# A windowed-attention and relu-squared kernel on one core: a new hand-written emission order, and the last pair's product and stores cut differently

## The chip, the core and the metric

The kernel runs on one NeuronCore of a Trainium2 chip. The metric is the device time of one execution in microseconds (us); lower is better. The core has TensorE (PE, matrix products; its weight loads are shown apart as PEld), VectorE (DVE), ScalarE (ACT), GpSimd (POOL) and SyncE (SP). SP, ACT and POOL can each issue DMAs, which all run on the core's 16 DMA engines.

## What is computed

Attention with a sliding window of 128 keys and 4 sink keys over 4 batches of 8 heads, 768 positions, head size 64; then a two-layer network with a squared relu:

```python
scores = where(keep, q @ k.T / sqrt(64), -1e9)      # keep: key < 4, or 0 <= query - key < 128
x = softmax(scores) @ v                             # [4*768, 512]: heads side by side
g = maximum(x @ w_in, 0) ** 2                       # w_in  [512, 2048]
out = g @ w_out                                     # w_out [2048, 512], out float32
```

## The kernel before

**Tiles and stages.** A batch is 6 tiles of 128 rows, taken as three pairs (256 rows). Per batch come: q and k turned so that the head size lies on the partitions (batches 0 and 1 by PE transposes, batches 2 and 3 by DMA transposes that SP issues, L389), scores (L529), exp on ACT (L549), masks (L558, L561 on DVE, L198 on POOL), sink scores and values (L490, L583), values (L608), the norm (L623, L624), x turned again (L653 or, for batches 2 and 3, L639), layer 1 (L685; in batches 2 and 3 `layer1_fast`, L825, with seven block products for eight), relu and square, and layer 2 (`layer2`, L914, for the first two pairs of batch 0; otherwise `layer2_fast`, L1024). `layer2_fast` makes the four quarters c, b, d and a of a pair's output from seven products of eight matmuls, with four block sums on DVE ahead of them (L982) and additions on the way out (L1049, L1065, L1072). The fast forms need sums of weight blocks: three `weights_in` into `qkT` (L735, free once all scores of batch 2 are done), two in place in `w_in_sb` (L730), and four of `w_out` (L955).

**What sets the order.** Nothing is scheduled by machine. `Plan` (L75) holds 898 numbered operations with the engines that each may run on. The string `ORDER` (L18 to L57) lists them once each; a word is an operation's number, the engine that it is given (p PE, v DVE, a ACT, g POOL, s SP) and, for some PE words, `+n`: so many dummy matmuls ahead (`warm`, L168 to L172). `Plan.run` (L87) emits the words one by one. Each engine works through its own words strictly in that order. An operation that takes a buffer gets the one that was freed first in the emission (`free[s.pool].pop(0)`), so the order also decides who shares a buffer with whom: 4 slots of two PSUM banks for products, 15 for middle results, 2 for output tiles.

**Words that the prediction speaks of** (the same number is the same operation before and after, up to 877):

| word | operation |
|---|---|
| 0, 1 | constants; zero and one fills of batch 0 (L213 to L215), which the v loads of batch 0 wait for |
| 3, 4, 5, 6 | identity, triangles, bias tiles, head rows (POOL, L224 to L249) |
| 8 to 15 | float32 loads of q and k of batch 0, issued by SP (L313) |
| 19, 20, 22, 23 | v loads of batch 0, tiles 0 to 3 (POOL, L339) |
| 21, 24, 25, 26 | the four quarters of w_in (POOL, L278); they arrive as bf16 |
| 27 to 30 | q and k of batch 0, tiles 4 and 5 (POOL, L328) |
| 74, 79 | a regroup of q (L182 on POOL, L181 on DVE or ACT); sink values (L473) |
| 119 | mask of batch 0, second pair |
| 160, 166, 172 / 163, 169, 175, 181 | layer 1 of batch 0, first pair / second pair, 16 matmuls each; 160 and 163 use the first quarter of w_in, 166 and 169 the second, 172 and 175 the third, 178 and 181 the fourth |
| 125, 127 | x of batch 0, second pair, turned |
| 229, 246, 294, 312, 270 | norm, mask (batch 1), evacuation, the first product of layer 2's third pair of batch 0, scores |
| 395, 421 | sink scores of batch 2; scores of batch 2 |
| 425, 606, 607 to 613 | mask of batch 2; loads of q, k and v of batch 3 |
| 477, 480 | copy u of batch 1's second pair (L1038 to L1043, helper L181); a product that waits for it |
| 506, 507, 508 / 509, 510 | `weights_in` into qkT / in place |
| 526, 527, 540, 541 | products that read 509 and 510 |
| 638, 654, 662 | scores of batch 3 |
| 863 to 877 | layer 2 of batch 3, second pair; 874 its last product, 875 the middle quarters, 876 the first quarter, 877 its store of 512 KB |
| 878 to 892 | layer 2 of batch 3, last pair ("tail"), up to its last quarter |

**The tail before.** Product a of the last pair (893) is 16 matmuls into two halves of a slot of its own. `first_quarter` (895, L1084) copies one half on DVE and the other on ACT, and issues a 64 KB store for each, from SP and from ACT. `store_rest` (896, L1102) issues the two middle quarters as two stores of 128 KB on SP; `store_last` (897, L1111) the last quarter, 128 KB, on SP. The second pair's store 877 stands ahead of 896 on SP.

Of the kernel before, what the change touches and what calls it, by code (L numbers as in the profile page):

```python
# [12 lines left out]
FP32 = mybir.dt.float32  # L13
# [2 lines left out]
ALU = mybir.AluOpType  # L16

ORDER = """  # L18
8s 0v 6g 4g 3g 9s 10s 11s 55v 5g 12s 13s 14s 56v 1v 19g 57p 59a 58p+3 60v 20g 21g 22g 67a 23g 103p+8 68v 61v 62v 7a
69p 71v 63p+1 70p 73v 72a 83p 85a 64p 104p 75p 107a 15s 74g 105a 65v 79g 66v 91p 93a 77v 76p 78v 80v 84p 86a 87p+1 92p  # L20
89p 94a 114p 116a 24g 25g 81p 82a 26g 27g 28g 88v 106v 95p 97p 115p 120p 129g 90v 99p 98v 96v 101p+1 29g 30g 117v 109p
118a 102v 110p 111v 121p 100a 160p 119v 123p 31g 32g 108v 33g 122v 124v 112p 113v 166p 125p 126a 127p 128v 172p 175p
173a 176v 177v 163p 164a 165a 169p 161v 133p 135a 134a 167v 170a 34g 181p 35g 147p 171v 149a 148p 151a 2v 182v 178p
179a 130p 132a 131a 36g 37g 38g 39g 40g 297p 298p 138p 152v 183a 139p 150v 142a 143v 136p 137a 299p 300p 301p 140a
141v 41g 42g 43g 44g 45g 46g 168a 47g 144p 153p 154p 155v 145p 146v 302p 303p 156p 48g 158p 159a 282v 305a 304p 49g
50g 51g 157v 184p 16s 283v 284v 285v 174v 187p 306a 162a 185a 52g 53g 188a 196p 212g 200p 201p 54g 363g 364g 197p 199v
208p 209p 210a 381s 203v 193p 202v 198v 211v 223p 194a 195v 186v 226a 189v 224a 225v 227v 190p 242p 191a 286p 204p
206v 205p 287p 207v 245a 243a 257p 258v 365g 366g 367g 234p 237a 238g 259v 288p 289p 235a 368g 369g 370g 371g 372g
373g 236g 180v 192v 254p 213v 308v 216p 217a 255v 256v 219a 290p 291p 262p 265a 307s 228p 292p 293p 263a 266g 214p
246v 309v 384s 310v 311v 229v 260p 374g 261a 382s 244v 218v 383s 386s 294v 295a 385s 264g 215a 312p 314a 313p 220v  # L30
239p 270p 273a 271a 274g 387s 240p 241v 375g 315p 318v 221p 222v 316p 267p 247p 248p 249v 230p 232p 233v 268p 319p
250p 269v 251v 252p 253v 317a 320p 231a 404p 405a 275p 17s 407a 376g 377g 378g 323p 272v 276p 321v 322v 336p 337a 388s
338a 277v 324v 325a 348p 339p 340a 349v 406v 278p 390s 280p 279v 281a 408v 330p 379g 380g 604g 605g 350a 331a 397p
398a 399v 606g 400a 393v 401v 391s 342p 343a 421p 422a 345p 346v 389s 392s 296s 409p 623s 333p 410v 347v 402p 403v
412s 424a 344a 411s 624s 326s 607g 625s 608g 609g 610g 611g 612g 425g 334a 341a 327p 328v 413p 416a 613g 18s 627s 332v
329a 335v 449v 468v 470v 450v 360p 361a 414a 415g 351p 352a 357p 358a 469v 471v 431p 432a 472p 473p 394v 434a 435g
362a 475p 433v 474v 478v 439p 442a 440a 395p 507v 396a 417g 508v 506v 476p 354p 477v 359a 426p 355a 511a 353a 356a
436p 437p 438v 451v 452v 479p 480p 418p 423g 427p 428v 514v 453p 455a 419p 420v 454p 456p 457p 622s 458a 638p 614g
512v 628s 641a 459v 629s 487v 639a 488v 481v 482v 483p 484v 640v 513v 460p 461p 626s 444p 462v 485a 463v 441g 642v
443g 615g 616g 635v 654p 657a 655a 445p 464p 446v 530p 532a 486s 465v 466a 531p 533v 509v 489v 662p 665a 534p 447s  # L40
429s 516p 517p 518v 491p 492p 494p 493a 535v 515v 430s 510v 490v 663a 448s 519v 617g 656g 520p 521v 536p 537p 495p
498p 496a 643p 497v 500v 644v 544v 546v 522p 658g 523p 618g 538a 540p 619g 633s 541p 542v 539a 524a 525a 499p 502p
526p 527p 543a 545v 501v 503v 630s 467s 547v 576p 562p 577p 528v 578a 579v 580p 563p 666g 634g 504a 564a 566p 590p
591p 565v 581v 567v 548p 550v 549p 568p 505s 592a 593v 582p 569p 583p 594p 529a 596p 551v 570a 572p 573p 584a 585a
690v 595v 597p 574v 552p 554p 553v 586p 587p 598a 599a 588v 632s 691v 555p 556a 620g 600p 631s 636p 637a 601p 575a
602v 664v 694p 558p 559p 645p 648a 692v 646a 560v 693v 695p 649v 697p 696a 700v 589a 667p 672p 675a 647v 668p 669v
698p 650p 651v 653s 603a 699a 701p 702p 703v 621g 673a 561v 571v 557a 704v 709v 680p 676g 681a 682g 710v 659p 674g
652s 705p 711v 660p 661v 683a 713p 715v 714p 716p 717p 712v 720p 706v 707a 719v 708s 684g 747a 718v 749v 748v 677p
685p 678p 679v 721p 686p 687v 766p 768a 752p 753p 722v 723v 728v 767p 770p 689s 754a 756p 729v 724p 755v 750v 757v
732p 733p 734a 758p 759p 769v 730v 731v 771v 671s 688s 772p 735p 773p 751v 760a 725v 726a 762p 763p 764v 736p 739p  # L50
738v 670s 780v 782v 783v 774a 776p 777p 737a 778v 798p 800a 799p 740p 741v 742v 801v 727s 784p 786a 785p 787v 743p
781v 744v 812p 813p 802p 761a 814a 745a 746s 788p 779v 826p 804p 803v 789v 765a 827p 775v 805p 790p 816p 815v 818p
840v 791p 806a 808p 809p 817v 841v 828a 819p 830p 810v 829v 831v 792a 842v 794p 795p 796v 820a 822p 823p 824v 793a
811a 832p 833p 834a 835a 844p 846v 843v 807a 845p 821v 847p 850v 849a 836p 837p 838v 825a 839v 797a 878v 879v 848p
851p 852p 855p 882p 883p 859v 853v 854v 860v 856v 857v 858s 885p 863p 864p 866p 884v 888v 880v 887a 865a 881v 886p
889p 861v 867p 862v 869v 891v 892v 897s 868v 870p 872v 873v 871p 874p 875v 876a 877s 890p 894v 893p 895v 896s
"""  # L57


# [47 lines left out]
def kernel(  # L107
# [851 lines left out]
    def layer2_fast(b, u):  # L959
# [48 lines left out]
            else:  # L1008
                touch((b, u), e, ins, HOME[name][0], alone=alone)

        def product(n, name, lhs, rhs, first, after, takes=(), reads=()):
            def run(e):
                if n == 0:
                    bank_t["y", b, u] = tile_of(bs, "py", [128, 2, 2, 256], FP32)
                if tail and n == 2:
                    bank_t["ya", b, u] = tile_of(ys, "ya", [128, 2, 2, 256], FP32)
                y = region(name)
                x = lhs if not isinstance(lhs, str) else t_[lhs]
                w_ = wt_sb[rhs] if isinstance(rhs, int) else rhs
                for c in range(2) if tail and name == "a" else (None,):  # L1020
                    for i in range(HB):
                        y_ = y if c is None else y[:, c, :]
                        r_ = w_[:, i, :] if c is None else w_[:, i, 128 * c:128 * c + 128]
                        ins = nc.tensor.matmul(y_, lhsT=x[:, i, :], rhs=r_, start=(first or tail and n == 2) and i == 0,  # L1024
                                               stop=i == HB - 1, skip_group_check=not (first or tail and n == 2))
                        use(name, e, ins, c)
# [38 lines left out]
            nc.vector.tensor_tensor(out=t_["x"], in0=t_["x"], in1=t_["u"], op=ALU.add)  # L1065
        P.group = ("ev", b, u)
        e4 = op("last_quarter", "dve", last_quarter, after=[ex, eu])
        p2 = product(6, "a", a12, w(1, 0), False, [u0] + high)

        def middle(e):  # L1070
            o, y = bank_t["osb", b, u], bank_t["y", b, u]
# [10 lines left out]
            return pairs[:, i, c0:c1]  # L1082

        def first_quarter(e):  # L1084
            o, y = bank_t["osb", b, u], region("a")
            if not tail:
                use("a", e, copy(e, o[:, 0, :], y))
                return
            h = tile_of(half_, "half", [128, 128], FP32)
            use("a", "dve", copy("dve", o[:, 0, 0:128], y[:, 0]), 0)  # L1090
            use("a", "act", copy("act", h, y[:, 1]), 1)
            nc.sync.dma_start(out=rows(0, 0, 128), in_=o[:, 0, 0:128])
            nc.scalar.dma_start(out=rows(0, 128, 256), in_=h)
        half_ = Slot("w2", 1)
        e1 = op("first_quarter", "dve" if tail else "act dve", first_quarter, takes=[half_] if tail else [],
                after=[p2, em], reads=[ys, os_] if tail else [bs])
# [5 lines left out]
        def store_rest(e):  # L1102
            o = bank_t["osb", b, u]
            if b not in FAST or not u:
                nc.sync.dma_start(out=pairs.rearrange("p i m -> p (i m)")[:, 256:768],
                                  in_=o[:, 1:3, :].rearrange("p c m -> p (c m)"))
                return
            for i in range(2):
                nc.sync.dma_start(out=rows(i, 256 - 256 * i, 512 - 256 * i), in_=o[:, 1 + i, :])

        def store_last(e):  # L1111
            nc.sync.dma_start(out=rows(1, 256, 512), in_=bank_t["osb", b, u][:, 3, :])
        if tail:
            op("store_rest", "sp", store_rest, after=[em, e4], dma=2.0)
            op("store_last", "sp", store_last, after=[e4], dma=2.0)
        else:
            op("store", "sp", store, after=[em, e1, e4], reads=[os_], dma=2.0)


# [107 lines left out]
```

## Time and profile before

| | |
|---|---|
| runs | 217.24, 217.24 and 215.4 us; median 217.24 us |
| the profiled execution | 216.34 us; its span in the trace is 214.6 us |
| granted TensorE clock | 1.0 in every slice |
| PE / DVE / ACT / POOL busy | 93% / 80% / 60% / 48% of the span |
| DMA | 26.09 MB moved, 122 GB/s on average |

A span starts with the first instruction and ends with the last. In rows of the timeline the first two numbers are start and length in us; a bracket at the end names the idle time ahead of the instruction on its engine and what ended it. "x8" means eight instructions merged. In rows of the DMA view the last number is the median time in us from a DMA's issue to its landing.

### The profile page before, as it was taken

The page shows a single profiled execution, that of the slowest core. Times are in us where ns is not written, and L with a number is a line of the kernel's source. Part 1 is how long each engine was busy: PE and PEld are TensorE (multiplying, and loading weights), DVE is VectorE, ACT ScalarE, POOL GpSimd, SP SyncE. Part 2 cuts the span into 40 slices and gives each one's busy share as a digit, 9 for nine tenths or more (in the row PEclk, how much of TensorE's full clock was granted, in tenths as well). Part 3 has the DMA queues.
Part 4 walks back from the last instruction along what each step waited for, and adds up shares of the span by engine and source line. Part 5 has one row for each costly group of instructions (what it writes and reads, how often), then busy time and mean ns, then how long its engine had stood idle before and what let it go on. Part 6 is the DMA issues. An engine that isn't in the chain of part 4 may idle for free.

```text
span 214.6 us, 5463 instructions
## 1 busy us (share of the span) xinstructions
PE 199.2 (93%) x2270; PEld 163.4 (76%) x2270; DVE 171.6 (80%) x311; ACT 128.2 (60%) x165; POOL 102.8 (48%) x139
## 2 busy tenths in 40 slices
PE   1887899999998999999989998999999999999991
PEld 1546898579754785459768888998887999998981
DVE  4887176396799685479898999989998989998971
ACT  2582159845866536978992755678962245695001
POOL 5799265498979999032599199000244000000000
PEclk9999999999999999999999999999999999999999
DMA  5999999999999999997527949980022340200204
GB/s 164 270 154 189 179 190 213 170 153 146 104 214 131 165 125 159 177 178 148 127 53 49 147 97 81 225 97 0 3 49 100 75 124 5 99 0 3 98 27 171
DMA packets 93881, 26.09 MB, mean 122 GB/s; under 512 B 86816, under 2 KB 91552, under 8 KB 93856
## 3 DMA queue, kind: packets, MB, share of 16 engines
q0 software_dynamic: 69248, 12.59, 78.3%
q1 hardware_dynamic: 24424, 13.07, 26.3%
q8 instruction: 18, 0.29, 0.5%
q10 hardware_dynamic: 184, 0.07, 0.1%
q14 instruction: 7, 0.06, 0.1%
HBM read 27.30 MB, written 6.29 MB: 156 GB/s over the span
## 4 chain that ended last, share of the span: by engine, by line
PE 68%; DVE 15%; DMA 6%; POOL 3%; issue 3%; ACT 2%; DVEq 0%; ACTq 0%
PE py L1024 20%; PE pm L685 17%; PE pm L825 15%; DMA w_in_sb<-in_moe_w_in_dram 5%; PE py L914 4%; PE po L608 4%; PE ps L529 4%; DVE sg L982 3%; PE pt L425 2%; POOL v L339 2%; DVE qkT L735 2%; DMA qr<-in_k_dram 1%; DVE w_in_sb L730 1%; DVE r L893 1%; DVE gT_sb L982 1%
## 5 line engine op out<-in xcount | busy, mean ns | idle before, releaser
L198 POOL TENSOR_SCALAR_AFFINE_SELECT expm<-expm 128x512 bf16<-128x512 bf16 x38 | 32.0, 876 | 43.8 <-ACT expm L549 43.8
L549 ACT ACTIVATE expm<-ps 128x1024 bf16<-128x1024 f32 (+1 forms) x48 | 43.8, 958 | 11.3 <-PE ps L529 11.1
L685 PE MATMUL pm<-xT,w_in_sb 128*128 128x256 bf16 (+1 forms) x320 | 44.6, 295 | 1.0 <-DMA w_in_sb<-in_moe_w_in_dram 1.0
L685 PEld LDWEIGHTS <-w_in_sb 128*128 128x128 bf16 x320 | 34.3, 114 | 7.7 <-DMA w_in_sb<-in_moe_w_in_dram 1.3
L1024 PEld LDWEIGHTS <-gT_sb 128*128 128x128 bf16 x336 | 30.8, 98 | 4.8 <-issue 1.2
L1024 PEld LDWEIGHTS <-sg 128*128 128x128 bf16 x240 | 22.4, 98 | 5.0 <-DVE xn_sb L624 1.2
L825 PE MATMUL pm<-xs,w_in_sb 128*128 128x128 bf16 (+1 forms) x256 | 24.0, 246 | 0.8 <-DVE w_in_sb L730 0.8
L696 ACT ACTIVATE r<-pm 128x1024 bf16<-128x1024 f32 x17 | 17.4, 1026 | 10.6 <-PE pm L685 10.4
L339 POOL DMA_DIRECT2D v<-in_v_dram x24 | 21.9, 923 | 2.6 <-DVE v L215 1.7
L825 PEld LDWEIGHTS <-w_in_sb 128*128 128x128 bf16 x256 | 21.7, 114 | 1.2 <-DVE w_in_sb L730 0.9
L1024 PE MATMUL py<-wt,sg 128*128 128x256 bf16 x160 | 20.8, 273 | 1.3 <-DVE xn_sb L624 0.9
L1024 PE MATMUL py<-wt,gT_sb 128*128 128x256 bf16 x160 | 20.8, 273 | 0.7 <-DVE u L181 0.7
L328 POOL DMA_DIRECT2D qn<-in_q_dram x20 | 17.8, 902 | 6.1 <-DMA w_out_sb<-in_moe_w_out_dram 5.3
L847 ACT ACTIVATE gT_sb<-r 128x1024 bf16<-128x1024 bf16 x18 | 18.7, 1057 | 0.3 <-DVE r L893 0.2
L179 ACT ACTIVATE osb<-py 128x256 f32<-128x256 f32 (+1 forms) x17 | 7.0, 420 | 19.7 <-DVE osb L1072 10.3
L1024 PE MATMUL py<-w_out_sb,gT_sb 128*128 128x256 bf16 x144 | 18.7, 273 | 0.0
L328 POOL DMA_DIRECT2D qn<-in_k_dram x20 | 17.8, 907 | 1.0 <-issue 1.0
L624 DVE TENSOR_TENSOR xn_sb<-po,rc 128x512 bf16<-128x512 f32 (+1 forms) x28 | 17.2, 615 | 1.0
L893 DVE CUSTOM_DVE_ANT_1 r<-pm,t 128x1024 bf16<-128x1024 f32 x12 | 14.6, 1220 | 2.7 <-PE pm L825 2.5
L881 ACT ACTIVATE r<-pm 128x1024 bf16<-128x1024 f32 x12 | 12.1, 1020 | 7.1 <-PE pm L825 7.0
L825 PEld LDWEIGHTS <-qkT 128*128 128x128 bf16 x192 | 16.1, 114 | 0.2 <-issue 0.2
L866 DVE TENSOR_TENSOR t<-t,pm 128x512 f32<-128x512 f32 x24 | 15.9, 680 | 0.3
(94 smaller groups left out, 328.8 us busy)
## 6 DMA issues: line engine op xcount, KB each, us to landing
out_dram<-osb SPq DMA_DIRECT2D x11, 512.0 KB, 4.6
v<-in_v_dram POOLq DMA_DIRECT2D x24, 128.0 KB, 6.1
qn<-in_k_dram POOLq DMA_DIRECT2D x20, 128.0 KB, 6.9
qn<-in_q_dram POOLq DMA_DIRECT2D x20, 128.0 KB, 6.5
w_in_sb<-in_moe_w_in_dram POOLq DMA_DIRECT2D x4, 512.0 KB, 9.3
w_out_sb<-in_moe_w_out_dram POOLq DMA_DIRECT2D x4, 512.0 KB, 10.5
qr<-in_k_dram SPq DMA_DIRECT2D x4, 256.0 KB, 4.9
qr<-in_q_dram SPq DMA_DIRECT2D x4, 256.0 KB, 4.7
```

The lines of the kernel that those rows point to most:

```text
L198: nc.gpsimd.affine_select(out=e_tile, in_=e_tile, compare_op=ALU.is_ge, fill=fill, base=i - 1, pattern=[[0, n], [1 if i else -1, 128]], ch ...
L328: nc.gpsimd.dma_start(out=qn_t[b, ti][:, t, :].rearrange("p (h d) -> p h d", d=D), in_=(q, k)[ti][b, :, 128 * t:128 * t + 128, :].rearrang ...
L339: nc.gpsimd.dma_start(out=v_sb[b % 2][:, t, :, 0:D], in_=v[b, :, 128 * t:128 * t + 128, :].rearrange("h p d -> p h d"))
L549: nc.scalar.activation(out=x[:, :, o:512], in_=bank_t["s", b, s, m][:, :, o:512], func=AF.Exp, scale=scale)
L624: touch(("po", b, s, m0), e, nc.vector.tensor_tensor(out=xn_sb[:, 2 * s:2 * s + 2, :].rearrange("p i (j q h d) -> q p j i h d", j=2, q=2, ...
L685: nc.tensor.matmul(pm[:, i, :], lhsT=w_in_sb[:, fb // 4, kb, fb % 4:512:4], rhs=xT[:, c0 // 256:(c0 + cw) // 256, kb, :], start=(kb == 0), ...
L696: nc.scalar.activation(out=o, in_=h, func=AF.Relu)
L825: touch(tag, e, nc.tensor.matmul(y[:, bk, i, :], lhsT=weights(name, f0 + i, a), rhs=rhs[:, a, :], start=fresh and i == 0 and a == 0, stop= ...
L847: nc.scalar.activation(out=d, in_=x, func=AF.Square)
L866: touch(tag, e, nc.vector.tensor_tensor(out=T["t"], in0=T["t"], in1=T["y"][:, bk], op=ALU.subtract), bk)
L893: touch(tag, e, nc.vector._custom_dve(TENSOR_ADD_SAT, out=r.rearrange("p b n c -> p b (n c)"), in0=T["y"].rearrange("p b n c -> p b (n c)" ...
L1024: ins = nc.tensor.matmul(y_, lhsT=x[:, i, :], rhs=r_, start=(first or tail and n == 2) and i == 0, stop=i == HB - 1, skip_group_check=not ...
```

## The change

The words of `ORDER` are put in another order over the whole kernel, and 77 operations below 878 go to another engine or carry another number of dummy matmuls (18 dummies in all, 14 before). Of the layer 2 code only the last pair changes: its last product becomes two operations (893, 894) of eight matmuls, one for each half; the halves are copied by an operation each (898, 900) into the output tile, and no longer into a tile of their own; the two middle quarters leave in one DMA of 256 KB (897); and each of the four stores may be issued by SP or ACT. The words that the prediction speaks of, engine by engine:

```diff
 POOL, start
-6g 4g 3g 5g 19g 20g 21g 22g 23g 74g 79g 24g 25g 26g 27g 28g 129g 29g 30g
+4g 3g 5g 6g 19g 20g 21g 22g 23g 24g 25g 26g 27g 28g 79g 119g 29g 30g
 DVE, start
-0v 55v 56v 1v 60v 68v 61v 62v
+0v 1v 55v 67v 59v 71v 60v 61v 72v 73v 65v 74v
 PE, start
-57p 58p+3 103p+8 69p 63p+1 70p 83p ... 160p 123p 112p 166p 125p 127p 172p 175p 163p 169p 133p 181p
+57p 69p+11 58p 70p+1 103p+1 83p ... 160p 110p 121p 112p 123p 166p 125p 127p 172p 163p 181p 169p 130p
 around 246 and 477
-246v ... 507v 508v 506v 477v
+246g ... 451v 508v 635v 507v ... 485v 506v   (and 477a, on ACT, behind 434a 396a 432a)
 ACT between 421p and 395p
+422a 424a 349a 279a 347a 337a 338a 361a 416a 352a 414a 511a 358a
 POOL, loads of batch 3
-606g 607g 608g 609g 610g 611g 612g 425g 613g
+606g 425g 607g 608g 609g 610g 611g 612g 613g
 PE, end
-837p 848p 851p 852p 855p 882p 883p 885p 863p 864p 866p 886p 889p 867p 870p 871p 874p 890p 893p
+837p 847p 848p 851p 852p 855p 882p 883p 885p 886p 889p 863p 864p 866p 867p 890p 893p 870p 871p 874p 894p
 DVE, end
-861v 862v 869v 891v 892v 868v 872v 873v 875v 894v 895v
+862v 865v 891v 892v 869v 895v 872v 873v 875v 876v
 ACT and SP, end
-865a 876a                    858s 897s 877s 896s
+868a 897a 898a 900a          858s 899s 896s 901s 877s
```

In the new order 895 is the middle quarters of the last pair, 896 the store of its last quarter, 897 that of its middle quarters, 898 and 900 the copies of the halves of product a, 899 and 901 their stores. The code:

```diff
-        p2 = product(6, "a", a12, w(1, 0), False, [u0] + high)
+        if tail:
+            p2s = [product(6, "a", a12, w(1, 0), False, [u0] + high, cs=(c,)) for c in range(2)]
+        else:
+            p2 = product(6, "a", a12, w(1, 0), False, [u0] + high)
...
+        def half(c):
+            def run(e):
+                use("a", e, copy(e, bank_t["osb", b, u][:, 0, 128 * c:128 * c + 128], region("a")[:, c]), c)
+            return run
...
+        def queue(e):
+            return nc.scalar if e == "act" else nc.sync
+
+        def store_middle(e):
+            o, two = bank_t["osb", b, u], rows(0, 256, 512)
+            two = bass.AP(two.tensor, two.offset, [list(two.ap[0]), [128 * DM - 256, 2], [1, 256]])
+            queue(e).dma_start(out=two, in_=o[:, 1:3, :])
...
         if tail:
-            op("store_rest", "sp", store_rest, after=[em, e4], dma=2.0)
-            op("store_last", "sp", store_last, after=[e4], dma=2.0)
+            op("store_last", "sp act", store_last, after=[e4], dma=2.0)
+            op("store_middle", "sp act", store_middle, after=[em], dma=2.0)
+            for c in range(2):
+                ec = op("half", "dve act", half(c), after=[p2s[c]])
+                op("store_half", "sp act", store_half(c), after=[ec], dma=2.0)
```

More of the change, by code (lines that the diff above doesn't have):

```diff
@@ L24 @@
[L24 to L28, printed above, removed]
@@ L57 @@
+863p 865v 864p 866p 868a 867p 891v 890p 893p 892v 870p 869v 871p 874p 895v 872v 897a 898a 899s 896s 894p 900a 901s
+873v 875v 876v 877s
 """
@@ L1019, in run @@
                 w_ = wt_sb[rhs] if isinstance(rhs, int) else rhs
-                for c in range(2) if tail and name == "a" else (None,):
+                for c in cs if tail and name == "a" else (None,):
                     for i in range(HB):
@@ L1084, in first_quarter @@
         def first_quarter(e):
[L1085 to L1096, printed above, removed]
+            use("a", e, copy(e, bank_t["osb", b, u][:, 0, :], region("a")))
+        def half(c):
+            def run(e):
+                use("a", e, copy(e, bank_t["osb", b, u][:, 0, 128 * c:128 * c + 128], region("a")[:, c]), c)
+            return run
         def store(e):
```

88 lines of the change are left out of this document (45 added, 43 removed).

## The prediction

> **What bounds the kernel now.** I read the page's head, the list of PE's waits, the timeline at each longer wait, then the DMA view around the loads concerned. First the page: span, busy time, and the share of each engine in the chain that ended last.
>
> ```profile
> span 214.6 us, 5463 instructions
> PE 199.2 (93%) x2270; PEld 163.4 (76%) x2270; DVE 171.6 (80%) x311; ACT 128.2 (60%) x165; POOL 102.8 (48%) x139
> PE 68%; DVE 15%; DMA 6%; POOL 3%; issue 3%; ACT 2%; DVEq 0%; ACTq 0%
> ```
>
> PE bounds it: 93% busy and 68% of the chain. The diff takes no product away, so PE's 199.2 us stay (four more dummies fall where PE waits), and only the rest, 214.6 − 199.2 = 15.4 us, can shrink. The list of PE's waits says where some of it lies (us in total, times, longest).
>
> ```profile
> PE pt L425 <- DVE qs L181: 4.8, 2, 4.6
> PE py L1024 <- DVE xn_sb L624: 0.9, 1, 0.9
> PE pm L825 <- DVE w_in_sb L730: 0.8, 1, 0.8
> PE py L1024 <- DVE u L181: 0.7, 1, 0.7
> ```
>
> 4.6 pass before the first k tile is cast; the diff leaves those loads alone. The other three sum to 2.4 us. The timeline of the start shows more.
>
> ```profile
> 3.79 1.29 DVE L181 CAST qs<-qr 128x512 bf16<-128x512 f32 x2 [2.14 <-DMA qr<-in_k_dram]
> 6.05 0.10 DVE L215 MEMSET v<- 128x48 bf16 x1
> 6.45 2.16 POOL L339 DMA_DIRECT2D v<-in_v_dram  x2 [1.66 <-DVE v L215]
> 9.35 1.80 POOL L339 DMA_DIRECT2D v<-in_v_dram  x2
> 11.71 1.81 POOL L473 TENSOR_TENSOR vs<-vs_in,head_rows 32x130 bf16<-32x130 f32 x4
> 13.47 2.31 POOL L278 DMA_DIRECT2D w_in_sb<-in_moe_w_in_dram  x3
> 16.03 1.02 ACT L549 ACTIVATE expm<-ps 128x1024 bf16<-128x1024 f32 x1 [0.21 <-PE ps L529]
> 21.98 1.94 PE L685 MATMUL pm<-xT,w_in_sb 128*128 128x256 bf16 x16 [0.89 <-DMA w_in_sb<-in_moe_w_in_dram]
> 24.52 7.18 PE L685 MATMUL pm<-xT,w_in_sb 128*128 128x256 bf16 x64 [0.15 <-DMA w_in_sb<-in_moe_w_in_dram]
> ```
>
> PE is dense only from 24.52 on: both bracketed waits end when a quarter of w_in lands. These quarters are issued by POOL at 13.47, 14.24 and 15.0 (the x3 row). So the kernel is a start set by loads, a dense run with a few stalls, and a tail.
>
> **The change part by part.**
>
> *The start.* Issue to landing, in the DMA view at 13.4, 15.7 and 10.2 us (last number, a median):
>
> ```profile
> w_in_sb<-in_moe_w_in_dram POOLq DMA_DIRECT2D x1, 512.0 KB, 8.5
> w_in_sb<-in_moe_w_in_dram POOLq DMA_DIRECT2D x1, 512.0 KB, 12.1
> v<-in_v_dram POOLq DMA_DIRECT2D x2, 128.0 KB, 7.9
> ```
>
> The second quarter lands at 13.47 + 8.5 = 21.97, the third at 24.5 (PE's wait), the fourth at 15.0 + 12.1 = 27.1: 2.5 apart, one transfer behind another. The last v load ahead of them (issued about 10.25) lands at 18.2, 3.77 before 21.97; 3.77 − 2.5 leaves a gap of about 1.2 in the stream. Two edits feed it earlier. First, 1v stands ahead of the casts on DVE, in the 2.14 us in which DVE has nothing to do; POOL, free at 6.45 − 1.66 = 4.79, can then issue v at once, 1.66 earlier. Second, 24g to 26g no longer stand behind 74 and 79g (2.3 us from 11.15 to 13.47), so they follow 23g directly: issued some 4 us earlier in all, ahead of need, and the gap closes. Upper bound of the gain: 1.66 + 1.2 = 2.9. Attention cuts it: the exp of the second pair ended at 17.05 and gets a regroup of about 0.6 ahead of it; its mask (119, now POOL, 1.2 to 1.8) ends near 19.2, its values, 166p (16 matmuls, 1.9) and the turn of x follow, so 172p starts no earlier than about 22.0: 24.52 − 22.0 = 2.5. Lower bound 0: v and w_in share the DMA engines with the q and k loads, and being issued earlier may bring nothing. A loss has one door: 119g blocks POOL ahead of 29g (a load of tile 5's q), priced at 0.65, the time POOL is late there. I take the whole gap and a third of the 1.66, which competes with q and k: −1.2 − 0.6 = **−1.8** (0.65 to −2.5). PE's new order 172p 163p 181p 169p uses the fourth quarter second but one; at 2.5 apart it lands 2.5 behind the third, and PE has 172p and 163p (3.8) to do meanwhile.
>
> *246 to POOL.* The timeline around 66 us:
>
> ```profile
> 62.96 0.68 DVE L561 TENSOR_TENSOR expm<-expm,tri 128x1024 bf16<-128x1024 bf16 x1
> 67.65 1.05 PE L1024 MATMUL py<-wt,sg 128*128 128x256 bf16 x8 [0.92 <-DVE xn_sb L624]
> 70.21 0.62 PE L529 MATMUL ps<-qkT 64*128 64x128 bf16 x12 [0.42 <-DVE osb L181]
> ```
>
> 312p waits 0.92 for a norm on DVE that stands behind masks of this form (0.68); 270p waits 0.42 for evacuation 294. With 246 on POOL, and evacuations moved to ACT, DVE is 0.7 to 1.1 earlier. Norm, evacuation, block sum and sink exp still follow each other, four steps of about 0.65 (0.68 in the row above), 2.6 us, beside two groups of eight products (1.05 each), 2.1 to 2.2, so 0.4 of 0.92 + 0.42 = 1.34 stays: **−0.9** (0 to −1.34).
>
> *477 to ACT, weights_in spread.* The three into qkT, then the one in place that PE waits for:
>
> ```profile
> 105.94 4.78 DVE L735 TENSOR_TENSOR qkT<-w_in_sb 128x2048 bf16<-128x2048 bf16 x3 [0.47 <-PE pk L490]
> 110.65 0.41 DVE L181 COPY u<-py 128x256 f32<-128x256 f32 x1
> 127.71 1.65 DVE L730 TENSOR_TENSOR w_in_sb<-w_in_sb 128x2048 bf16<-128x2048 bf16 x1
> 129.41 0.64 PE L825 MATMUL pm<-xs,w_in_sb 128*128 128x128 bf16 x8 [0.78 <-DVE w_in_sb L730]
> ```
>
> 477 stood behind those 4.78 us, and PE waited 0.7 for it. On ACT it is behind 434, 396 and 432 alone: **−0.7** (0, if ACT is as late, to −0.7). The in-place pair is read two layer 2 products (1.7 us of PE) earlier than before, when it was already 0.78 late: 2.5 must be found on DVE. 477 and seven evacuations of its length have left DVE since (8 × 0.41 = 3.3), though not all of that was ahead of need; 3.3 − 2.5 is too near to book: **0** (−0.78 to +1.0).
>
> *New waits.* 395p (sink scores, batch 2) needs an evacuation that stands behind 13 ACT operations. ACT's pace there, first and last of three:
>
> ```profile
> 98.35 1.01 ACT L696 ACTIVATE r<-pm 128x1024 bf16<-128x1024 f32 x1
> 100.15 1.03 ACT L696 ACTIVATE r<-pm 128x1024 bf16<-128x1024 f32 x1
> ```
>
> 0.9 from start to start: 13 take 11.7 to 12 us. Between 421p and 395p PE has five layer 1 products (16 of the x64 in 7.18, so 1.75), two of layer 2 (0.87) and three small ones (0.5): 12.0. On DVE, 515v waits for 511 on ACT and holds all behind it. Zero margin on both sides: **+0.5** (0 to +1.1).
>
> *Tail.* PE's last products, the last two stores of 128 KB, their landing, and the landing of the 512 KB store (its own, then smallest, median and largest of nine):
>
> ```profile
> 209.26 1.06 PE L1024 MATMUL ya<-w_out_sb,gT_sb 128*128 128x128 bf16 x16
> 209.46 0.69 DVE L1072 TENSOR_TENSOR osb<-py,u 128x512 f32<-128x512 f32 x1 [0.18 <-PE py L1024]
> 210.76 1.24 SPq L1109 DMA_DIRECT2D out_dram<-osb  x2
> DMA to landing us min/median/max: 2.6/2.6/2.6
> out_dram<-osb SPq DMA_DIRECT2D x1, 512.0 KB, 2.9
> DMA to landing us min/median/max: 2.9/4.5/4.9
> ```
>
> PE ends at 210.32; the last 128 KB is issued at 211.5 and lands at 214.1, PE's end + 3.8. In the new order 874p ends 0.45 before PE does; its 875v (0.69) and 876 (0.4) let 877, 512 KB, go last on SP, at PE's end + 0.75 to 0.9 behind the last quarter's issue. Landing in 2.9 gives + 3.65 to 3.8; in 4.9, + 5.7. That store had nothing behind it but small ones before, as now, so I take 2.9: **+0.1** (−0.3 to +1.9). PE's order there hides each DVE chain behind 4 to 5 us of products as before: 0 (0 to +0.6). The one store of 256 KB for two of 128 saves an issue on SP that nothing waits for: 0; a second queue for the last stores: 0, as the issue rows of 0.4 to 0.7 are all it could hide.
>
> [...]
>
> *Other engine swaps*: evacuations between DVE and ACT, either with room at those places: 0; if the cover goes, one evacuation is 0.4 to 0.7.
>
> Sum: −1.8 − 0.9 − 0.7 + 0 + 0.5 + 0.1 = −2.8. The profiled execution took 216.34 (span 214.6 + 1.74 around it), so 213.5; the median of the runs, 217.24, is 0.9 above the profiled one, and I stay with its own time.
>
> **The rivals.** *A: the DMA engines, not POOL's issue, time w_in*; or another order's new waits eat what it saves. Then the start gains 0.8 at most, and 216.34 − 0.8 − 0.9 − 0.7 + 0.5 + 1 = 215.9. For it: the quarters land 2.5 apart although issued 0.77 apart, so the stream is full. Against: the gap of 1.2.
>
> *B, slower: loads of batch 3 behind a mask.* POOL at 92 us, the landing of a load at 86 to 90 us, the transposes on SP, and the scores of batch 3:
>
> ```profile
> 92.47 1.22 POOL L198 TENSOR_SCALAR_AFFINE_SELECT expm<-expm 128x512 bf16<-128x512 bf16 x2 [6.09 <-ACT expm L549]
> 93.64 0.90 POOL L328 DMA_DIRECT2D qn<-in_q_dram  x1
> qn<-in_q_dram POOLq DMA_DIRECT2D x1, 128.0 KB, 11.7
> 102.83 6.46 SPq L389 DMA_TRANSPOSE qkT<-qn  x5
> 120.15 0.60 PE L529 MATMUL ps<-qkT 64*128 64x128 bf16 x12
> ```
>
> Before, mask 425 ran at 92.47 with one load behind it; POOL had idled 6.09 us for its exp. Now 607g to 613g all stand behind it: seven issues of 0.9 end near 100, land up to 11.7 later (112), and up to five transposes (1.3 each, 6.5) follow, 118 and more with their landing. The scores that need them begin at 120.15, or about 117 with the gains above. In the bad corner PE waits 3 to 5: 216.5 to 218.5, and with the new waits at their bound of 1.1 up to 219. It decides once the last turned tile lands more than 2.8 us after 117. Against: 11.7 was measured with many loads in flight; a spread stream should land sooner.
>
> *C: the 512 KB store, now last, lands in 4.9* instead of 2.9: 213.5 + 1.9 = 215.4. Against: its own row, 2.9, in the same neighbourhood.
>
> *D: POOL issues slower beside DVE's casts.* The two v issues at 6.45, beside casts, took 1.08 each, the two at 9.35 took 0.90, so 0.18 each is what the rows bear out; if the earlier issues lost the whole of the start's 1.8, 215.3. [...]
>
> **How the numbers follow.** The forecast 0.52, A 0.25, B 0.10, C 0.08, D 0.05. About 1% (2.2 us) is what a measurement of this kernel can tell from no change. The forecast's own range is 211.2 (start at its bound −2.5, stalls at theirs, −0.9 and −0.7 more) to 214.6 (start at −0.7). A, C and D end at 215.3 to 216.3 and are in the range to 216.8; B beyond it and the ends below 211.2 are left out, less than 2 in 10. Faster by over 1%, below 214.2: 0.47 of the forecast's 0.52 and 0.04 of A and C, where the stalls go whole, 0.51; within 1%: the rest of the forecast, of A and C, D, and a fifth of B, 0.41; slower by over 1%, above 218.5: B at its worst, together with new waits at their bound, 0.08.
>
> **What would show it.** Right: 16 matmuls of L685 that wait for w_in start near 22.7 in place of 24.52; v issues on POOL begin near 4.8; no wait of L1024 on `u` and at most 0.4 near 66 us; the last store is issued within 0.9 of PE's end and lands in about 3. Wrong: a PE wait for `qkT` at 117 to 122 (B); w_in quarters that still land at 22.0 and 24.5 (A); a PE wait on ACT near the sink scores of batch 2, or on `w_in_sb` L730, of over 1 us; or PE's waits for DVE grown in many small pieces between 105 and 205 us that no single step here names.

## The result and the profile after

The changed kernel takes 214.80 us (median of 20 runs, 212.96 to 215.40), the kernel before 216.06 (20 runs, 214.79 to 217.82). The ratio is 0.9916, 95% interval 0.9888 to 0.9945: faster by 0.84%. The interval leaves out 1, so the gain is real; its middle lies inside the 1% that the prediction counts as no change. The two medians alone are 1.26 us (0.58%) apart. The profiled execution of the changed kernel took 215.08, with a span of 213.3; that of the kernel before took 216.34 and 214.6.

The page's head after: span, busy time, shares of the chain. Lines of the code are one higher than before up to the tail.

```profile
span 213.3 us, 5447 instructions
...
PE 200.8 (94%) x2270; PEld 164.8 (77%) x2274; DVE 175.2 (82%) x307; ACT 126.3 (59%) x165; POOL 103.6 (49%) x144
...
PE 82%; DVE 9%; DMA 2%; ACT 2%; issue 1%; SPq 1%; DVEq 0%; ACTq 0%
```

PE is busy 1.6 us longer with the same products, and idle 2.9 us less (12.5 against 15.4). The longer work turns out to be slow matmuls at the start (PE is 18.5 busy up to 24.11; it was 16.6 up to 24.52). PE's waits after:

```profile
PE pt L426 <- DVE qs L182: 4.6, 2, 4.2
PE py L1025 <- DVE sg L983: 0.7, 1, 0.7
PE pm L826 <- DVE xs L784: 0.6, 1, 0.6
PE pm L826 <- DVE w_in_sb L731: 0.5, 1, 0.5
```

The waits for w_in, for the norm near 66 us, for `u` and for `osb` ahead of 270p are gone; a wait for xs (128x512 halves of x) and one for a block sum `sg` are new.

The timeline of the start after:

```profile
4.84 2.00 POOL L340 DMA_DIRECT2D v<-in_v_dram  x2
...
9.31 2.44 POOL L279 DMA_DIRECT2D w_in_sb<-in_moe_w_in_dram  x3
...
13.32 0.61 PE L530 MATMUL ps<-qkT 64*128 64x128 bf16 x6
...
17.75 1.02 ACT L550 ACTIVATE expm<-ps 128x1024 bf16<-128x1024 f32 x1
...
18.91 1.67 POOL L199 TENSOR_SCALAR_AFFINE_SELECT expm<-expm 128x512 bf16<-128x512 bf16 x2 [3.23 <-ACT expm L550]
...
20.77 1.30 PE L609 MATMUL po<-v,expm 128*128 128x65 bf16 x32
...
21.91 1.92 PE L686 MATMUL pm<-xT,w_in_sb 128*128 128x256 bf16 x16
...
24.11 6.06 PE L686 MATMUL pm<-xT,w_in_sb 128*128 128x256 bf16 x54
```

and the landing of w_in's second quarter, issued at 9.31:

```profile
w_in_sb<-in_moe_w_in_dram POOLq DMA_DIRECT2D x1, 512.0 KB, 9.1
```

The reader is to see two things. The loads came early as forecast: v from 4.84, the quarter at 9.31 + 9.1 = 18.4 in place of 21.97. And 172p (the first pair's products with the third quarter of w_in) still starts at 24.11, only 0.41 before its old 24.52, because the exp of the second pair (17.75 + 1.02) ends at 18.77; in the kernel before it ended at 17.05.

From 172p on, the same PE work remains in both kernels, since the set of PE words ahead of 172p is the same. So a kernel's span splits cleanly: when 172p starts, and what comes from there to the end. Before: 24.52 + 190.08. After: 24.11 + 189.19. The change gained 0.41 at the start and 0.89 behind it.

The windows view of 66 to 70 us, before and then after (length, then busy time of PE, PEld, DVE, ACT, POOL, PE clock, DMA share, GB/s):

```profile
66.00:70.00 4.00, 2.87 (x30) 1.77 (x29) 3.97 (x6) 1.77 (x5) 4.00 (x5) 1.00 2.11 159
```

```profile
66.00:70.00 4.00, 4.00 (x64) 3.21 (x58) 3.96 (x7) 3.36 (x6) 3.99 (x6) 1.00 0.81 75
```

PE goes from 2.87 busy to 4.00: the whole stall is gone, while DVE is as full as before.

The new waits, and the last products and stores, in the timeline after:

```profile
125.61 3.02 DVE L731 TENSOR_TENSOR w_in_sb<-w_in_sb 128x2048 bf16<-128x2048 bf16 x2 [0.91 <-PE pm L826]
...
128.68 1.53 PE L826 MATMUL pm<-xs,w_in_sb 128*128 128x128 bf16 x24 [0.53 <-DVE w_in_sb L731]
...
129.39 2.14 DVE L784 TENSOR_TENSOR xs<-xT 128x512 bf16<-128x512 bf16 x3
...
130.81 0.63 PE L826 MATMUL pm<-xs,qkT 128*128 128x256 bf16 x4 [0.60 <-DVE xs L784]
...
193.53 1.99 ACT L848 ACTIVATE gT_sb<-r 128x1024 bf16<-128x1024 bf16 x2
...
195.55 0.69 DVE L983 TENSOR_TENSOR sg<-gT_sb 128x1024 bf16<-128x1024 bf16 x1 [0.81 <-ACT gT_sb L848]
...
196.30 1.05 PE L1025 MATMUL py<-wt,sg 128*128 128x256 bf16 x8 [0.67 <-DVE sg L983]
...
208.13 0.61 PE L1025 MATMUL ya<-w_out_sb,gT_sb 128*128 128x128 bf16 x8
...
209.51 0.38 SPq L1098 DMA_DIRECT2D out_dram<-osb  x1
```

The two in-place `weights_in` (3.02 us together) now run back to back, and xs stands behind them. The sum at 195.55 waits for two squares on ACT. At the end, the 512 KB store goes last, 0.77 after PE's end at 208.74; the span ends 4.56 after PE, before 4.28.

### The profile page after: what moved, and what is told of

Its sections match the earlier page's. It is cut to its first block, busy times and chain, and to the rows that moved or that the text cites. A ratio compares the mean times of both kernels' runs of the same rounds, so it can differ in the third digit from the quotient of the medians.

```text
span 213.3 us, 5447 instructions
## 1 busy us (share of the span) xinstructions
PE 200.8 (94%) x2270; PEld 164.8 (77%) x2274; DVE 175.2 (82%) x307; ACT 126.3 (59%) x165; POOL 103.6 (49%) x144
## 4 chain that ended last, share of the span: by engine, by line
PE 82%; DVE 9%; DMA 2%; ACT 2%; issue 1%; SPq 1%; DVEq 0%; ACTq 0%
PE py L1025 22%; PE pm L686 19%; PE pm L826 17%; PE py L915 7%; PE ps L530 6%; PE po L609 4%; PE pt L426 3%; DMA qr<-in_q_dram 2%; DVE qkT L736 1%; DVE w_in_sb L731 1%; DVE sg L983 1%; PE px L654 1%; PE ps L523 1%; PE po L584 1%; DVE xn_sb L625 1%
## 5 line engine op out<-in xcount | busy, mean ns | idle before, releaser
L199 POOL TENSOR_SCALAR_AFFINE_SELECT expm<-expm 128x512 bf16<-128x512 bf16 x40 | 30.7, 798 | 49.4 <-ACT expm L550 49.3
L848 ACT ACTIVATE gT_sb<-r 128x1024 bf16<-128x1024 bf16 x19 | 19.2, 1058 | 4.4 <-DVE r L894 4.3
L697 ACT ACTIVATE r<-pm 128x1024 bf16<-128x1024 f32 x14 | 14.3, 1024 | 12.5 <-PE pm L686 12.1
L882 ACT ACTIVATE r<-pm 128x1024 bf16<-128x1024 f32 x12 | 11.9, 1022 | 10.0 <-PE pm L826 9.3
L699 DVE TENSOR_SCALAR r<-pm 128x1024 bf16<-128x1024 f32 x10 | 12.3, 1228 | 5.4 <-PE pm L686 5.4
```

What stands on the lines that cost most here:

```text
L199: nc.gpsimd.affine_select(out=e_tile, in_=e_tile, compare_op=ALU.is_ge, fill=fill, base=i - 1, pattern=[[0, n], [1 if i else -1, 128]], ch ...
L848: nc.scalar.activation(out=d, in_=x, func=AF.Square)
```

## The experiments

Every kernel here is either the changed kernel or the kernel before with words of `ORDER` edited; all compute the full output. The results first, so that they can be held side by side: where the exp of batch 0's second pair ends, where 172p starts, and what follows.

| kernel | exp ends | 172p | 172p − exp | span | from 172p to the end | ratio to before (95%) |
|---|---|---|---|---|---|---|
| before | 17.05 | 24.52 | 7.47 | 214.6 | 190.08 | 1 |
| after | 18.77 | 24.11 | 5.34 | 213.3 | 189.19 | 0.9916 (0.9888–0.9945) |
| e1_warm | 17.96 | 23.30 | 5.34 | 212.4 | 189.10 | 0.9923 (0.9885–0.9961) |
| e2_mask_v | 17.16 | 22.96 | 5.80 | 212.7 | 189.74 | 0.9942 (0.9904–0.9980) |
| e3_old_front | 18.79 | 23.76 | 4.97 | 212.9 | 189.14 | 0.9965 (0.9927–1.0003) |
| e4_loads | 17.82 | 22.80 | 4.98 | 212.9 | 190.10 | 0.9982 (0.9937–1.0026) |
| e5_prewarm | 17.03 | 22.36 | 5.33 | 211.5 | 189.14 | 0.9872 (0.9820–0.9924) |
| e6_246g | 17.96 | 22.93 | 4.97 | 211.9 | 188.97 | 0.9896 (0.9842–0.9949) |
| e7_477a | 18.63 | 23.60 | 4.97 | 212.9 | 189.30 | 0.9968 (0.9928–1.0007) |
| e8_prewarm_before | 17.45 | 23.07 | 5.62 | 213.2 | 190.13 | 0.9931 (0.9901–0.9962) |
| e9_sum | 17.60 | 22.58 | 4.98 | 210.6 | 188.02 | 0.9823 (0.9773–0.9873) |
| e10_tail | 18.72 | 24.05 | 5.33 | 213.5 | 189.45 | 0.9946 (0.9912–0.9980) |
| e11_mid | 18.61 | 23.94 | 5.33 | 212.1 | 188.16 | 0.9867 (0.9818–0.9915) |
| e12_mended | 16.77 | 22.11 | 5.34 | 209.7 | 187.59 | 0.9822 (0.9775–0.9869) |

The times of 172p and of the exp are from one profiled execution each, in us; a ratio is over several runs (6 to 20 of the kernel) against the kernel before run beside it. Read the columns: "from 172p to the end" repeats within 0.1 us between kernels that differ only in the start (190.08, 190.10, 190.13; 189.19, 189.10, 189.14, 189.14), while the start moves by over a microsecond between executions of the same words: e6 and e7 are the kernel before up to 172p, and have it at 22.93 and 23.60, not 24.52. One row with only the start changed, e2, stands out with 189.74: a wait of 0.29 for a norm is back in it near 66 us. So a step behind 172p can be read from one profile to a few tenths, once its waits are compared; a step at the start can not.

**Is PE's slow start the cause? e1_warm** (changed kernel):

```diff
-57p 69p+11 ... 70p+1 ... 103p+1
+57p 69p+15 ... 70p+6 ... 103p+1
```

> Changed kernel with nine more dummy matmuls in the first 8 us (15 in place of 11 ahead of 69p, 6 in place of 1 ahead of 70p), so that PE has no pause between 4.2 and 8 us. In the changed kernel a 128x128 matmul takes about 0.1 us until 13.4 us, in the kernel before only until about 8.4. Theory 1 (the start lost its gain because PE ran slowly for 5 us longer, so scores and exps came late): the fast matmuls begin near 8.5 us, the exp of the second pair ends about 1 us earlier, 172p starts at 23.1 in place of 24.1, and the ratio to the kernel before goes from 0.992 to about 0.987. Theory 2 (the mask on POOL and the exps set the start, whatever PE's speed): fast matmuls earlier, but 172p still at 23.8 to 24.1, ratio 0.991 to 0.992.

In the profile 172p started at 23.30 and the fast matmuls began between 9.4 and 10.6 (6 products of 64x128 in 0.61 at 9.36, 4 of 64x256 in 0.34, not 0.50, at 10.61). The trace fits theory 1; the ratio, 0.9923, does not move from 0.9916. So nine more dummies in these places are not shown to shorten the runs.

**Is it the mask on POOL? e2_mask_v** (changed kernel, `119g` → `119v`).

> Changed kernel with mask 119 (batch 0, second pair) on DVE again in place of POOL. In the changed kernel that mask takes 1.67 us on POOL and the values of 123p start as it ends (20.6). Theory 2 (mask on POOL sets the start): on DVE it takes 0.7 to 0.9, so 166p and 172p start 0.8 to 1.0 earlier (172p at 23.2), ratio 0.988. Theory 1 (PE's late speed-up is the cause): the exp ahead of the mask is late either way, DVE does its other two masks behind this one, and 172p moves by 0.3 at most: ratio 0.990 to 0.992.

172p at 22.96, but with an exp that ended at 17.16: the distance grew to 5.80, because PE waited 0.48 for x on DVE that now does that mask too. Its ratio, 0.9942, is no better. 172p came earlier only because the exp did, 1.61 us in this execution, which the mask's place can't cause: the mask comes behind the exp. So theory 2 falls. What goes with the early exp is PE's speed. The words up to the exp are those of the changed kernel, whose profile has 0.61 for these six at 8.59 and for six others still at 13.32; here they are fast:

```profile
8.34 0.40 PE L530 MATMUL ps<-qkT 64*128 64x128 bf16 x6 [0.21 <-DVE qkT L182]
```

So the moment of the speed-up differs between executions of the same words, and the exp's end with it: 17.16 here, 17.96 with fast products by 10.61 (e1), 18.61 by 11.68 (e11), 18.77 after 13.32 (changed kernel).

What the new words between exp and 172p cost, the mask on POOL among them, is 0.36: 5.33 in the rows with the new start, 4.97 in those with the old one.

**What is the new start worth? e3_old_front** (words up to 172p as before, then the new order).

> Changed kernel, but with the words of the kernel before up to the word 172p (engines, dummies and order), then the remaining words in the new order. The set of PE work ahead of 172p is the same in both. If the start is worth the 0.4 us that the traces show (172p at 24.11 against 24.52): 172p at 24.5, the later gains kept, ratio 0.993 to 0.994. If the start were worth the 1.8 that was forecast: ratio 1.000. If the later gains hang on the start (DVE or DMA earlier all along): the waits near 66 us come back, ratio above 0.996.

0.9965 against 0.9916: by these ratios the new start is worth about 0.5% (1 us). But the two intervals overlap, and by the quotients of the medians (215.58 to 216.34, and 214.80 to 216.06) it is 0.2%, so its worth is not settled. The later gain stays whole without it (189.14), and the waits near 66 us are not in e3's list. So the rival that it hangs on the start falls, although the ratio lies where that rival had put it.

**The loads alone: e4_loads** (kernel before):

```diff
-0v ... 56v 1v ... 23g ... 74g ... 79g ... 24g 25g 26g 27g
+0v 1v ... 56v ... 23g 24g 25g 26g ... 74g ... 79g ... 27g
```

> Kernel before with only the two edits of loads at the start: the fills 1v ahead of the casts on DVE, and the w_in issues 24g to 26g directly behind 23g, ahead of 74g and 79g. PE speeds up as early as before and mask 119 stays on DVE. By the forecast's step: v issues begin at 4.8, w_in quarters land about 3.5 us earlier, 172p starts at 22.0 to 22.7 and the ratio is 0.988 to 0.992. Rival A (DMA engines set the arrival): w_in lands at most 1 us earlier, ratio 0.996 to 1. Rival C (74g and 79g, now later, are themselves on the way: their regroup delays the third pair's scores and the sink values): 172p not earlier than 24, ratio 1.0 or above.

```profile
4.98 1.93 POOL L339 DMA_DIRECT2D v<-in_v_dram  x2
...
9.46 2.25 POOL L278 DMA_DIRECT2D w_in_sb<-in_moe_w_in_dram  x3
...
20.60 1.92 PE L685 MATMUL pm<-xT,w_in_sb 128*128 128x256 bf16 x16
...
22.80 7.15 PE L685 MATMUL pm<-xT,w_in_sb 128*128 128x256 bf16 x64
```

The profile does what the forecast's step says to a tenth: v at 4.98, no w_in wait, 172p at 22.80, time 214.6, 1.74 below the profiled execution of before. Yet over 12 runs the ratio is 0.9982, with its interval around 1. Both are true: in the profiled execution of before w_in bound the start, but in e6 and e7, where POOL issues it just as late (13.44 and 12.96), it landed in time. The DMA view of the second quarter's landing in e6, and PE there:

```profile
w_in_sb<-in_moe_w_in_dram POOLq DMA_DIRECT2D x1, 512.0 KB, 6.7
```

```profile
20.73 1.92 PE L685 MATMUL pm<-xT,w_in_sb 128*128 128x256 bf16 x16
...
22.93 1.04 PE L685 MATMUL pm<-xT,w_in_sb 128*128 128x256 bf16 x8
```

6.7 us in place of 8.5, and no bracket: no wait for w_in. The runs of e4 still reach 217.42, as those of the kernel before do, so late w_in isn't what makes the long runs.

**PE kept busy from the first moment: e5_prewarm** (changed kernel) **and e8_prewarm_before** (kernel before):

```diff
 e5
-57p 69p+11 ... 70p+1
+57p+16 69p+15 ... 70p+6
 e8
-57p
+57p+16
```

> Changed kernel with 16 dummy matmuls ahead of PE's first product (from 2.5 us, when the identity tile is ready), 15 in place of 11 ahead of 69p and 6 in place of 1 ahead of 70p: PE works without a pause from 2.5 to 8 us. Up to now the moment at which a 128x128 matmul goes from 0.107 to 0.056 us differed from run to run (8.5 to 13.5 us), and the end of the second pair's exp with it (17.05 to 18.8). Theory 3 (this moment makes the two groups of times of one kernel, near 213.0 and 214.9 for the changed one, and it hangs on PE's first pauses): fast matmuls by 7 us, exp of the second pair ends at 17.2 or earlier, 172p at 22.5, the times fall together near 213.0, ratio 0.984. Rival (the groups come from the arrival of the q, k and w_in loads): fast matmuls early, but exps still wait for late loads, two groups remain, ratio 0.990 to 0.993.

> Kernel before with only 16 dummy matmuls ahead of PE's first product. Theory 3 (two groups of times, near 215.2 and 217.5, come from the moment at which PE speeds up): fast matmuls by 7 to 8 us, the upper group is gone, ratio 0.995. Rival (the upper group comes from w_in landing late, which this doesn't touch): 172p still waits for w_in at 24 to 25 in part of the runs, both groups remain, ratio 1.000.

Scores of batch 0 in the timeline, changed kernel with early dummies:

```profile
8.89 0.40 PE L530 MATMUL ps<-qkT 64*128 64x128 bf16 x6 [0.41 <-DVE qkT L182]
...
9.65 0.34 PE L530 MATMUL ps<-qkT 64*128 64x256 bf16 x4
```

Six products of 64x128 take 0.40 here and 0.61 in the changed kernel at 13.32. The exp ends at 17.03 in place of 18.77, 172p comes at 22.36, and the ratio is 0.9872. PE was not quite without a pause: it waited 1.16 ahead of 7.10 for a cast. On the kernel before, the 16 dummies alone give 0.9931; its runs lie between 214.41 and 215.67, where those without lie between 214.62 and 217.83. In e8 w_in is then what ends last (PE waits 0.21 for it ahead of 172p, distance 5.62). For the kernel before the runs do what theory 3 says: the long ones vanish, although w_in is issued nearly as late as before (in the DMA view its quarters are being issued from 13.2 to 15.6, and none at 9.8 to 11.8). But no profile here caught a long execution, so that PE's speed-up comes late in them is argued, not seen. For the changed kernel theory 3 holds in part: five of six runs at 212.7 to 213.7, one at 214.96 remains; 0.9872 lies between the 0.984 of theory 3 and the 0.990 of its rival, and its interval overlaps that of the changed kernel. Something else also varies, which these runs don't name.

**246 alone (e6_246g) and 477 alone (e7_477a)** (kernel before, `246v` → `246g`; `477v` → `477a`).

> Kernel before with only mask 246 on POOL. By the forecast's step 0.9 of the 1.34 us of PE's waits near 66 to 70 us go (312p's wait for the norm, most of 270p's for evacuation 294), ratio 0.996. Rival (the mask must be off DVE together with the evacuations, or POOL is too late with it): the waits stay or go elsewhere, ratio 1.000. This run also gives a second look at the start of the kernel before, which is unchanged here: if w_in's landing time differs from run to run, its second quarter lands more than 0.5 us from 21.97.

> Kernel before with only copy u (477) on ACT in place of DVE. By the forecast's step PE's wait of 0.70 at 111 us for u goes, ratio 0.997. Rival (ACT does it behind its other work just as late, or the wait moves to the next product that needs DVE, which still has the 4.8 us of weights_in ahead): the same 0.5 to 0.7 shows at another line, ratio 1.000. A third look at the start of the kernel before.

246 on POOL takes 1.11 us off what follows 172p (190.08 to 188.97), and neither wait near 66 us is left in e6's list. The products there:

```profile
65.05 1.05 PE L1024 MATMUL py<-wt,sg 128*128 128x256 bf16 x8
...
67.29 0.62 PE L529 MATMUL ps<-qkT 64*128 64x128 bf16 x12
```

No brackets: 312p and 270p wait for nothing. (The ratio of the six runs, 0.9896, is lower than the 0.995 that 1.11 us would make; with a start that varies by over a microsecond they don't say why.) 477 on ACT takes 0.78 off (to 189.30); its wait doesn't come back on another line. Together 1.89, twice what the whole new order gained there (0.89). The ratio of 477 alone, 0.9968 (0.9928 to 1.0007), is not clear of no change; its 0.78 is read from the profiles.

**The tail's order: e10_tail** (changed kernel; 870 871 874 and 877 ahead of the last pair's, as before; 876 also goes from DVE to ACT, as it had been).

> Changed kernel with its last 27 words in the older sequence: products 870, 871, 874 of the second pair ahead of 890, 893, 894, its evacuation and its 512 KB store ahead of the last pair's stores. In the changed kernel the span ends 4.56 us after PE's last product (before: 4.28), with the 512 KB store issued last, 0.77 after PE's end. If that place of the store costs time: it is issued at or ahead of PE's end, the last store is one of 128 KB, and the span ends 3.3 to 4.0 after PE's last product: 0.6 to 1.2 us less, ratio 0.987 to 0.989. If the stores run together at the DMA engines' rate whatever their order: 4.3 to 4.6 as now, ratio 0.991.

```profile
207.61 1.06 PE L1025 MATMUL ya<-w_out_sb,gT_sb 128*128 128x128 bf16 x16
...
210.73 0.41 SPq L1113 DMA_DIRECT2D out_dram<-osb  x1
```

The 512 KB store went early (208.12), but ACT's two copies of the last product came late (209.50), the last small store went at 210.73, and the span ended 4.83 after PE (208.67), not 3.3 to 4.0. My expectation failed. Since products, copies and stores all moved, this run doesn't single out the place of the 512 KB store; that it alone costs the tail's 0.28 isn't borne out, and where the 0.28 lies stays open.

**The two new waits: e11_mid** (changed kernel):

```diff
-494p 509v 526p 538a 510v 527p 540p 644v 541p 545v 544v
+494p 545v 509v 526p 538a 510v 527p 540p 644v 541p 544v
-839v 849a 848p 851p 852p 855p 811v 853v 797a 807a 878v 879v
+839v 797a 807a 849a 848p 851p 852p 855p 811v 878v 853v 879v
```

> Changed kernel with two places of its DVE and ACT order mended: xs (545v) ahead of the two in-place weights_in, in DVE's 0.91 us of idle time, and two squares (797, 807) ahead of a copy on ACT with the sum 878 ahead of 853 on DVE. In the changed kernel PE waits 0.60 us for xs at 130.8 and 0.67 us for a block sum at 196.3. If these two are the new waits that eat the change's later gain: both shrink below 0.2, from 172p to the span's end goes from 189.2 to 188.1 to 188.5, ratio 0.987. Rival (DVE is so full there that the wait moves to the next product): the same time under other lines, 189.0 or more, ratio 0.991.

Both waits are gone from the list, and what follows 172p is 188.16, 1.03 less than 189.19. Ratio 0.9867. DVE had room; its order had not used it. One wait of the kind that 246 had taken away is back in this execution, as in e2:

```profile
66.67 1.05 PE L1025 MATMUL py<-wt,sg 128*128 128x256 bf16 x8 [0.28 <-DVE xn_sb L625]
```

**Sums of the parts: e9_sum** (kernel before with 57p+16, 1v, 24g to 26g, 246g, 477a) **and e12_mended** (changed kernel with e5's dummies and e11's two edits).

> Kernel before with five edits and nothing else of the change: 16 dummies ahead of 57p, fills 1v early, 24g to 26g behind 23g, 246 on POOL, 477 on ACT. If the parts add up: the exp of the second pair ends near 16.5, 172p starts at 21.6 to 22.3 with no wait for w_in; from 172p to the span's end 190.1 - 1.13 (measured with 246 alone) - 0.78 (477 alone) = 188.2; span 210, time near 212, ratio 0.980. That would be better than the whole new order with early dummies (0.987). If the new order's other moves carry a gain of their own, or 246 and 477 share one wait: from 172p on 189 or more, ratio 0.984 or above.

> Changed kernel with early dummies (16 ahead of 57p, 15 ahead of 69p, 6 ahead of 70p) and with the two mended places of its DVE and ACT order together. If start and dense run add up independently: 172p at 22.4 (as with the early dummies alone), from there to the span's end 188.2 (as with the mended places alone), span 210.5, time 212.2, ratio 0.982, as good as five edits on the kernel before. If an earlier start brings later waits forward (DVE or DMA then late): from 172p on 188.8 or more, ratio 0.985 or above.

e9: 188.02 from 172p on (expected 188.2), the exp's end at 17.60 and 172p at 22.58 (later than the 16.5 and the 21.6 to 22.3 expected), median 212.31. e12: 22.11 + 187.59, median 211.81 (211.07 to 212.40), the lowest of all kernels here; its ratio, 0.9822, can't be told from e9's 0.9823. Behind 172p it is 0.6 better than the 188.2 expected; 0.28 of that is the norm's wait that e11's execution has and this one hasn't, and the rest isn't traced. Its waits of 0.2 us and more behind 172p:

```profile
PE pm L826 <- DVE w_in_sb L731: 0.5, 1, 0.5
PE po L584 <- DVE osb L182: 0.2, 1, 0.2
```

Five edits of the old order reach what the rewritten order reaches once mended, as far as these intervals can tell.

## Why the prediction's time lay in its range, and where its steps failed

The forecast was 213.5 with 211.2 to 216.8; 214.80 lies inside. It lies above the forecast's own range, though, which ended at 214.6; it is inside because the range was widened for the rivals, so that is partly luck. The sign was right and the size was not: −2.8 forecast, −1.26 by the medians, so the likeliest class, faster by over 1%, was not the one that came. Of the signs named, v at 4.8, no wait on `u` and at most 0.4 near 66 us, and a last store within 0.9 of PE's end all came; products of L685 near 22.7 did not.

- **Start, −1.8 forecast, −0.41 measured** in the profiled pair. This is the step that failed. Its first half held: POOL issued v at 4.84 and w_in at 9.31, and w_in landed 3.6 us earlier. Its second half, "172p starts no earlier than about 22.0", was two microseconds off. The exp ended at 18.77, not 17.7, since PE ran its scores slowly until after 13.32 (6 products in 0.61, as at 8.59; six of them took 0.40 at 15.96). And from the exp to 172p there are 5.34 us (mask 1.67, values 1.30, 166p 1.92, the turn and the handovers), where I had left 4.3: 0.67 too little even for the old order (4.97 in e3, e6 and e7), and 0.37 for its new words. Both errors are 1.04 to 1.07, together the 2.1. No edit of the new start need have made PE slow for longer, since the moment differs between executions of the same words: six scores took 0.40 at 8.34 in e2 but 0.61 at 13.32 in the changed kernel; in the old order 0.40 at 9.52 in the kernel before, but 0.61 at 11.16 in e3, whose exp ended at 18.79. The 17.05 on which the forecast built was that of an execution with an early speed-up.
- **What the forecast was measured against.** The profiled start of before, 24.52, bound by w_in, was one sample. The same words gave 22.93 and 23.60 in e6 and e7. The term was sized on a wait that isn't in every run.
- **66 to 70 us, −0.9 forecast**: all 1.34 of PE's wait went; 246 alone accounts for 1.11 of the way to the end. The mechanism was right; of the "0.4 stays" nothing stayed in the profiled pair, and 0.29 and 0.28 in e2 and e11.
- **477, −0.7**: right, 0.78 alone.
- **Second weights_in, 0**: the wait went from 0.78 to 0.53, as near to nothing as booked; but xs, queued behind the back-to-back pair on DVE, was late by 0.60. I had not listed what is queued behind the pair.
- **New waits, +0.5 forecast, +1.27 measured**, and not where I looked. 395p, with my zero margin, waits for nothing in the list after; xs (0.60) and the sum `sg` behind ACT's squares (0.67) are the ones. e11 took them away and got 1.03 back, with 0.28 of the norm's wait back near 66 us.
- **Tail, +0.1 forecast, +0.28 measured** (4.56 against 4.28). The store of 512 KB was issued 0.77 after PE's end, in the forecast's 0.75 to 0.9. The view gives no landing for it, but the span ends 3.79 after its issue, so rival C, a landing of 4.9, didn't come.

The terms behind 172p sum to −1.34 − 0.70 − 0.25 + 1.27 + 0.28 = −0.74; the profiled pair shows −0.89, and 0.15 lies in pieces too small to name.

**Rival A**, 215.9: its first half didn't come, as w_in did land early and attention took its place as the bound. Its second half did: the start gained less than the 0.8 that it allowed, and the new order's own waits, 1.27 against the 1 that it put there, ate more than half of the 2.29 that went. **Rival B** didn't come. The mask ran at 91.67 and the loads of batch 3 followed it as priced, yet the scores at 117.39 had no wait:

```profile
97.19 1.80 POOL L329 DMA_DIRECT2D qn<-in_q_dram  x2
...
97.13 15.17 SPq L390 DMA_TRANSPOSE qkT<-qn  x6
...
117.39 0.62 PE L530 MATMUL ps<-qkT 64*128 64x128 bf16 x12
```

The last transposes were issued by 112.3, and the DMA view gives 2.5 us to landing for those, so they had landed by 114.8, over two microseconds ahead of need. **Rival D** didn't come either: the two v issues at 4.84 took 1.00 each (before: 1.08 and 0.90), and w_in was issued early as forecast, at 9.31. That the issues could lose the whole 1.8 was the author's estimate, and no run shows it. It was a mild test, as DVE was idle until a cast of 0.43 at 5.94 and copies from 6.28.

## What to carry to other kernels

Split the span at a point ahead of which the same work lies in both kernels, and read the two halves apart: here the second half repeats to a few tenths of a microsecond and can be judged from one profile with its list of waits, while the first differs by over 1 us from run to run and needs many. Before a wait for a load is booked as a gain, ask what ends next behind it and walk that chain with every product and handover on it; the load is only worth the gap to that chain. When an order by hand brings two long operations together on a nearly full engine, list what is queued behind them: moving a few words there (e11) was worth 1.03 us.

## What the runs showed of the hardware

In the first 14 us of these profiles a PE product of one form took one of two times (six of 64x128 0.61 or 0.40), and the granted clock is 1.00 with both: windows of 8 to 14 us, changed kernel and then the same with early dummies and mended places (length; PE busy and its matmuls; ...; granted PE clock after POOL's):

```profile
8.00:14.00 6.00, 6.00 (x46) 3.13 (x47) 4.38 (x9) 3.74 (x6) 5.94 (x9) 1.00 1.68 211
```

```profile
8.00:14.00 6.00, 5.99 (x79) 3.25 (x78) 5.60 (x12) 5.46 (x8) 5.94 (x9) 1.00 1.69 205
```

Both are busy all the time at a granted clock of 1.00; one does 46 matmuls, the other 79. At the slow speed 11 dummies took 1.38 (changed kernel) and 15 took 1.81 (e1), so one more takes about 0.107; at the fast one 4 products of the same form took 0.40 and 8 took 0.62 (kernel before), about 0.055 each. Without early dummies, the change of speed came between about 7.3 us (kernel before) and 13.9 us (changed kernel) in the profiles here. With PE busy from 2.54 us on (e12), the fast products are there by 8.6 (six of 64x128 in 0.40 at 8.59). With PE pausing for 0.4 us at 6.0 and again at 7.6, the changed kernel was slow for more than nine microseconds after its first product at 4.21. With the same words and a pause of 0.36 at 6.0, e2 had fast products by 8.34 (six in 0.40); what sets the moment is not shown.

In these rows masks took longer where DVE and POOL ran them at the same time. In the changed kernel POOL's two took 1.67 at 18.91 beside DVE's, and 1.22 at 91.67 where DVE ran no mask (1.22 at 92.47 in the kernel before). DVE's two took 2.01 at 19.11 beside POOL's, and 1.28 at 18.13 in e2, where POOL ran no mask.
